# A three-stage layer on one core: outputs stored tile by tile, the split of the moved blocks one tile later, a fourth buffer for them

## The chip, the cores and the metric

The kernel runs on one core of one Trainium2 chip. The metric is device time in microseconds, the median of several runs. A profiled execution has a time of its own, and every duration below comes from that one execution.

The engines go by the names of the profile: PE multiplies matrices (PEld is its weight load), DVE, ACT and POOL work on tiles of 128 partitions, and SP issues the DMAs. An engine runs its instructions in program order and waits at one until the semaphores that it names are reached.

## What is computed

The input `x` is 8 sequences of 3072 tokens with 256 numbers each, 24576 tokens in all. Three stages follow each other:

```python
X = np.fft.rfft(x, axis=1)                  # stage 1: mix in the frequency domain, soft threshold
...                                         # Y = shrink(X @ (w_r + i w_i) + b), back by irfft
d = softmax over tokens of (x @ phi)        # stage 2: 32 slots, 8 experts
slot_out[e] = np.maximum(slot_input[e] @ w1[e], 0.0) @ w2[e]
x = c @ slot_out                            # c: softmax over the 32 slots, per token
h = x @ w_in                                # stage 3, per token: 256 -> 1024
sm = softmax(h)
solu = h * sm
ln = (solu - mean) / np.sqrt(var + 1e-06) * g_ln
out = ln @ w_out                            # 1024 -> 256
```

Everything is float32. The change lies in stage 3.

## The kernel before

Function `phase1` does stages 1 and 2 up to the slots, some 650 us of the span. Function `phase2` first makes the experts' outputs and multiplies them into `w_in`, so that one matrix `gst` leads from a token's 32 slot weights to its 1024 numbers `h`. Its main loop then goes over the tokens in 192 tiles of 128 tokens (`NI` = 192, four tiles to a group `j`, eight tiles to a new block `ct` of slot weights).

Nothing reorders the instructions: each engine gets them in the order in which the Python loop calls its helpers. Step `i` of the loop works on several tiles at once, and this is who does what to a tile `t`:

- `hmat` (PE, two matmuls): `h` of the tile, into the PSUM tile `hps` (three buffers).
- `rowmax` (DVE, L990), `expo` (ACT, L997), `umul` (DVE, L1005): row extremum, exponential, and `u = h * e`.
- `blocks` (L1016 to L1026): the product with `w_out` needs `u` transposed. DVE transposes the 32x32 blocks of `u` into `tb` (L1021, three buffers), and then four DMAs on SP's queue, 128 KB each, move blocks between partitions into `t2` (L1025, three buffers; the profile calls it `t`). This is done for tile `i+1` in step `i`.
- `uhi` (ACT takes six eighths, L1061; POOL the other two, L1062) makes the high part `uh` of the moved blocks, and `ulo` (POOL, two halves, L1071) the low part `ul = t2 - uh`. Both have four buffers. In step `i` they work on tile `i-1`.
- `vari` (ACT, L1081): sum of squares. `rstd` (POOL, four small instructions, L1106 to L1109): the inverse deviation, once for four tiles, in the last group once for each tile. It stands between the two halves of `ulo`.
- `prod` (PE): 16 matmuls with `uh`, then 8 with `ul`, into a PSUM tile that holds two tiles (two buffers). In step `i` it works on tile `i-3`.
- `outp` (ACT, L1123): scales the product of tile `i-6` into a quarter of `osb` (two buffers of four tiles). `store` (L1134) issues the 512 KB DMA of a whole group, with runs of 4 KB, two steps after the group's last `outp`. The last group goes out tile by tile from `outp` itself (L1126).
- `late_c`: in every eighth step four DMAs load the next `ct` (L855). `last_c`, between steps 20 and 33, splits the last sequence's slot weights once.

The last two tiles (`direct`) are transposed by PE and have no blocks moved.

On SP's queue the loop therefore has, per tile, four DMAs for `t2`; per four tiles one store; per eight tiles four loads of `ct`. SP issues them one after the other, and the four for tile `i+1` wait both for DVE's transposition and for the `t2` buffer, which `ulo` of an earlier tile gives free.

Of the kernel before, what the change touches and what calls it, by code (L numbers as in the profile page):

```python
# [8 lines left out]
F32 = mybir.dt.float32  # L9
# [26 lines left out]
def kernel(  # L36
# [32 lines left out]
    NI = T // 128  # L69
# [769 lines left out]
    def phase2(p2: ExitStack, pw: ExitStack):  # L839
# [87 lines left out]
        v = psl.rearrange("p d (o s) -> p d o s", o=1).to_broadcast([128, 2, 4, 32])  # L927
# [10 lines left out]
        for fh in range(2):  # L938
            o = gst.rearrange("p (b c j) -> p b c j", b=4, c=8)[:, :, 4 * fh:4 * fh + 4]
            v = pg[fh].rearrange("p (c j b) -> p b c j", c=4, b=4)  # L940
# [5 lines left out]
        def right(name, bufs, **k):  # L946
            return p2.enter_context(tc.tile_pool(name=name, bufs=bufs, side="right", **k))

        e_p = right("e_p", 2)
        u_p = right("u_p", 4)  # L950
# [20 lines left out]
        def hmat(i):  # L971
            if i >= NI:
                return
            j, k = divmod(i, 4)
            ps = ph_p.tile([128, DFF], F32, name="hps", tag="hps")
            for fh in range(2):
                mm(ps[:, 512 * fh:512 * fh + 512], ctt[j][:, 128 * k:128 * k + 128], (gstn if direct(i) else gst)[:, 512 * fh:512 * fh + 512])
            hps[i] = ps
# [7 lines left out]
        def rowmax(i):  # L986
            if i >= NI:
                return
            st, k = stats(i)
            DVE.tensor_reduce(out=st[:, 0, k:k + 1], in_=hps[i], op=ALU.min, axis=AX.X)  # L990

        def expo(i):
            if i >= NI:
                return
            st, k = stats(i)
            e = e_p.tile([128, DFF], F32, name="e", tag="e")
            ACT.activation(out=e, in_=hps[i], func=AF.Exp, bias=st[:, 0, k:k + 1], scale=-1.0, accum_out=st[:, 1, k:k + 1])  # L997
            et[i] = e

        def umul(i):  # L1000
            if i >= NI:
                return
            st, k = stats(i)
            u = u_p.tile([128, DFF], F32, name="u", tag="u")
            DVE.scalar_tensor_tensor(out=u, in0=hps.pop(i), scalar=1.0, in1=et.pop(i), op0=ALU.mult, op1=ALU.mult, accum_out=st[:, 2, k:k + 1])  # L1005
            ut[i] = u


        def direct(i):
            return i >= NI - 2  # L1010

        def gst_order():
            POOL.tensor_copy(out=gstn.rearrange("p (c j b) -> p b c j", c=8, b=4), in_=gst.rearrange("p (b c j) -> p b c j", b=4, c=8).bitcast(F32))
# [3 lines left out]
        def blocks(i):  # L1017
            if i >= NI or direct(i):
                return
            t = u_p.tile([128, DFF], F32, name="tb", tag="tb", bufs=3)  # L1020
            DVE.transpose(out=t, in_=ut[i])  # L1021
            t2 = u_p.tile([128, 4, 256], F32, name="t2", tag="t2", bufs=3)
            for a in range(4):
                z = slice(32 * a, 32 * a + 32)
                SP.dma_start(out=t2[:, a, :], in_=t[z].rearrange("i (b x) -> i b x", b=4))  # L1025
            t2t[i] = t2  # L1026

        def trans(i):
            if i >= NI or not direct(i):
                return  # L1030
            ps = ph_p.tile([128, 8, 128], F32, name="pu", tag="hps")
            for c in range(8):
                tp(ps[:, c, :], ut[i][:, 128 * c:128 * c + 128])
            ut[i, 0] = ps

        def parts(i):
            uh = u_p.tile([128, 8, 128], F32R, name="uh", tag="uh")
            ul = u_p.tile([128, 8, 128], F32R, name="ul", tag="ul")
            uht[i] = (uh, ul)
            return uh, ul  # L1040

        def direct_parts(i):
            if i >= NI or not direct(i):
                return
            uh, ul = parts(i)
            ps = ut.pop((i, 0))
            for n in range(2):
                z = slice(4 * n, 4 * n + 4)
                ACT.activation(out=uh[:, z, :], in_=ps[:, z, :], func=AF.Copy)
                DVE.tensor_tensor(out=ul[:, z, :], in0=ps[:, z, :], in1=uh[:, z, :].bitcast(F32), op=ALU.subtract)  # L1050
# [4 lines left out]
        def uhi(i):  # L1055
            if i < 0 or direct(i):
                return
            uh, ul = parts(i)
            v = t2t[i].rearrange("p a (c j) -> p c a j", c=8)
            w = uh.rearrange("p c (a j) -> p c a j", a=4)  # L1060
            ACT.activation(out=w[:, 0:HA], in_=v[:, 0:HA], func=AF.Copy)  # L1061
            POOL.tensor_copy(out=w[:, HA:8], in_=v[:, HA:8])  # L1062

        def ulo(i, n):
            if i < 0 or direct(i):
                return
            uh, ul = uht[i]
            z = slice(4 * n, 4 * n + 4)
            v = t2t[i].rearrange("p a (c j) -> p c a j", c=8)[:, z]
            w = uh[:, z, :].rearrange("p c (a j) -> p c a j", a=4)  # L1070
            POOL.tensor_tensor(out=ul[:, z, :].rearrange("p c (a j) -> p c a j", a=4), in0=v, in1=w.bitcast(F32), op=ALU.subtract)  # L1071
            if n:
                t2t.pop(i)


        def vari(i):
            if i >= NI:
                return
            st, k = stats(i)
            sq = e_p.tile([128, DFF], F32, name="sq", tag="sq", bufs=1)  # L1080
            ACT.activation(out=sq, in_=ut.pop(i), func=AF.Square, bias=st[:, 2, k:k + 1], scale=-float(DFF), accum_out=st[:, 3, k:k + 1])  # L1081
# [29 lines left out]
        o_todo = {}  # L1111

        def outp(i):
            if i < 0:
                return
            j, k = divmod(i, 4)
            b, r = divmod(j, 6)
            h, ah = divmod(r, 2)
            v = out.rearrange("(b h lm a) d -> b h lm a d", b=B, h=3, a=8)[b, h, :, 4 * ah:4 * ah + 4, :]
            if k == 0:  # L1120
                osb[0] = o_p.tile([128, 4, D], F32, name="osb", tag="osb")
            o = osb[0]
            ACT.activation(out=o[:, k], in_=pot.pop(i), func=AF.Copy, scale=stt[j][:, 4, k:k + 1])  # L1123
            if j == NG - 1:

                SP.dma_start(out=v[:, k, :], in_=o[:, k, :])  # L1126
            elif k == 3:
                o_todo[i + 2] = (v, o)


        def store(i):
            if i in o_todo:
                v, os2 = o_todo.pop(i)
                SP.dma_start(out=v, in_=os2)  # L1134
# [4 lines left out]
        def last_c(i):  # L1139
            d = [c_dram[B - 1, k].rearrange("h s x -> (h s) x") for k in range(2)]  # L1140
            if i == 20:
                cl[0] = o_p.tile([96, 1024], F32R, name="cl", tag="cl", bufs=1)
                cl[1] = o_p.tile([96, 1024], F32R, name="cl_h", tag="cl_h", bufs=1)
                SP.dma_start(out=cl[0].bitcast(F32), in_=d[0])
            elif i in (24, 26, 28, 30):
                z = slice(128 * (i - 24), 128 * (i - 24) + 256)
                POOL.tensor_copy(out=cl[1][:, z], in_=cl[0][:, z].bitcast(F32))
                POOL.tensor_tensor(out=cl[0][:, z], in0=cl[0][:, z].bitcast(F32), in1=cl[1][:, z].bitcast(F32), op=ALU.subtract)
            elif i == 33:
                SP.dma_start(out=d[0], in_=cl[1].bitcast(F32))  # L1150
                SP.dma_start(out=d[1], in_=cl[0].bitcast(F32))
# [3 lines left out]
        def late_c(i):  # L1155
            if i in c_todo:
                load_c(*c_todo.pop(i))
# [10 lines left out]
        expo(1)  # L1168
        umul(0)
        blocks(0)  # L1170
        for i in range(NI + 6):
            j, k = divmod(i, 4)
            hmat(i + 3)
            trans(i)
            rowmax(i + 2)
            umul(i + 1)
            blocks(i + 1)
            store(i - 6)
            late_c(i)
            last_c(i)  # L1180
            outp(i - 6)
            vari(i)
            expo(i + 2)
            direct_parts(i)
            if i <= NI:
                uhi(i - 1)
                ulo(i - 1, 0)
            rstd(i)
            if i <= NI:
                ulo(i - 1, 1)  # L1190
            if i == 40:
                gst_order()
            if k == 1:
                pieces(j + 2)
            prod(i - 3)
# [142 lines left out]
```

## Time and profile before

| | us |
|---|---|
| median of 3 runs | 1372.1 (1368.52 to 1372.83) |
| profiled execution, its own time | 1369.07 |
| its span, first to last instruction | 1367.2 |
| main loop: transposition of tile 1 to that of tile 189 | 679.4 (661.70 to 1341.11) |
| DVE busy from 900 to 1000 | 97.2 |

The span is 1.9 us shorter than the execution's time, and that time is 3.0 us under the median of the runs. The numbers of the page are one execution's; a share of busy time is an average, so the main loop is read by itself, from about 662 to 1341 us.

### The profile page before, as it was taken

The numbers are of one execution on the slowest core, as the hardware profiler recorded it, in microseconds if no ns is written. First come the engines' busy times: TensorE is split into PE (matmuls) and PEld (weight loads), VectorE is DVE, ScalarE is ACT, GpSimd is POOL, SyncE is SP. The second block draws the span as 40 slices with busy tenths as digits, with TensorE's granted clock in tenths as the row PEclk, the third lists the DMA queues.
The fourth block names the chain that finished last, engine by engine and source line by source line (L and its number), as shares of the span: only waits on it lengthen the run. The fifth ranks groups of instructions, "written<-read, shape, count | busy, mean of one in ns | idle before, by whom it ended". The sixth has DMA issues, their size and how long they took to land.

```text
span 1367.2 us, 30896 instructions
## 1 busy us (share of the span) xinstructions
PE 1267.8 (93%) x10784; PEld 1126.7 (82%) x10784; DVE 1204.8 (88%) x1691; ACT 1038.8 (76%) x2005; POOL 978.6 (72%) x1045
## 2 busy tenths in 40 slices
PE   6999999999999999878699989999999999999998
PEld 3888888888888788754588879889888898888998
DVE  7787989797888889765899999999999999999994
ACT  5567676666666665533799989999899899899996
POOL 5556575756565654321488999999989899899996
PEclk8999999999999999989899999999999999999999
DMA  8965463646455463169478787878878788887874
GB/s 264 301 202 168 128 201 102 201 116 191 134 161 153 143 178 136 62 208 305 101 179 217 188 215 196 206 194 214 200 195 202 195 200 214 199 207 193 201 192 129
DMA packets 190746, 252.70 MB, mean 185 GB/s; under 512 B 21504, under 2 KB 155392, under 8 KB 190592
## 3 DMA queue, kind: packets, MB, share of 16 engines
q1 hardware_dynamic: 190256, 249.57, 67.1%
q8 instruction: 85, 1.39, 0.4%
q10 hardware_dynamic: 336, 1.18, 0.3%
q14 instruction: 69, 0.57, 0.1%
HBM read 91.94 MB, written 59.11 MB: 110 GB/s over the span
## 4 chain that ended last, share of the span: by engine, by line
PE 33%; DVE 14%; POOL 13%; DMA 13%; issue 11%; SPq 10%; ACT 5%; POOLq 0%; ACTq 0%; DVEq 0%
DMA t<-tb 9%; POOL ul L1071 8%; PE pb L89 7%; SPq L1025 7%; PE po L89 5%; PE pm L89 5%; PE s L89 4%; PE xps L89 4%; PE pa L89 3%; SPq L855 2%; PE sps L92 2%; POOL uh L1062 2%; DVE u L1005 1%; DVE sl L313 1%; ACT uh L1061 1%
## 5 line engine op out<-in xcount | busy, mean ns | idle before, releaser
L1071 POOL TENSOR_TENSOR ul<-t,uh 128x512 fp32r<-128x512 f32 x380 | 487.3, 1301 | 31.1 <-ACT uh L1061 30.6
L89 PEld LDWEIGHTS po<-gw,uh 128*128 128x128 f32 x3072 | 385.9, 190 | 78.7 <-ACT osb L1123 69.6
L89 PE MATMUL po<-gw,uh 128*128 128x256 f32 x3072 | 405.0, 285 | 40.5 <-ACT osb L1123 40.0
L343 POOL TENSOR_TENSOR s<-yb,s 128x512 f32<-128x512 f32 x95 | 132.3, 1392 | 217.4 <-DVE s L342 190.2
L1021 DVE STREAM_TRANSPOSE tb<-u 128x1024 f32<-128x1024 f32 x190 | 236.7, 1246 | 7.0 <-DMA t<-tb 0.4
L1005 DVE SCALAR_TENSOR_TENSOR u<-hps,e 128x1024 f32<-128x1024 f32 x192 | 232.3, 1210 | 11.5 <-ACT e L997 11.3
L990 DVE TENSOR_REDUCE st<-hps 128x1 f32<-128x1024 f32 x192 | 227.7, 1186 | 2.1 <-PE hps L89 2.1
L1081 ACT ACTIVATE sq<-u,st 128x1024 f32<-128x1024 f32 x192 | 221.2, 1152 | 0.2 <-DVE u L1005 0.2
L997 ACT ACTIVATE e<-hps,st 128x1024 f32<-128x1024 f32 x192 | 214.2, 1116 | 7.6 <-DVE st L990 6.9
L89 PE MATMUL po<-gw,ul 128*128 128x256 f32 x1536 | 214.2, 282 | 1.0 <-POOL ul L1071 1.0
L89 PEld LDWEIGHTS po<-gw,ul 128*128 128x128 f32 x1536 | 196.5, 190 | 1.4 <-POOL ul L1071 1.4
L1061 ACT ACTIVATE uh<-t 128x768 fp32r<-128x768 f32 x190 | 160.5, 845 | 43.0 <-DMA t<-tb 40.6
L235 POOL TENSOR_TENSOR x<-xc,x 96x512 fp32r<-96x512 f32 x120 | 162.6, 1364 | 31.4 <-ACT x L234 31.3
L89 PE MATMUL hps<-gst,ct 128*128 128x512 f32 x380 | 119.7, 398 | 12.0 <-DVE u L1005 10.6
L261 ACT ACTIVATE asb<-s 96x512 f32<-96x512 f32 x112 | 66.7, 595 | 73.8 <-PE s L89 71.2
L89 PE MATMUL s<-x,df_h 96*96 96x512 f32 x240 | 104.6, 438 | 13.1 <-ACT x L234 4.6
L1062 POOL CAST uh<-t 128x256 fp32r<-128x256 f32 x190 | 76.9, 405 | 51.6 <-DMA t<-tb 48.3
L89 PEld LDWEIGHTS xps<-d_sb,apt 128*128 128x128 f32 x768 | 99.0, 193 | 13.6 <-issue 2.9
L89 PE MATMUL xps<-d_sb,apt 128*128 128x128 f32 x768 | 105.1, 280 | 1.8 <-DMA apt<-ad 1.5
L1123 ACT ACTIVATE osb<-po,st 128x256 f32<-128x256 f32 x192 | 89.6, 468 | 11.4 <-PE po L89 8.3
L297 DVE TENSOR_TENSOR xsum<-xps,xi 128x256 f32<-128x256 f32 x96 | 39.8, 414 | 52.4 <-ACT xh L296 46.3
L234 ACT ACTIVATE x<-xc 96x512 fp32r<-96x512 f32 x120 | 75.2, 626 | 12.5 <-DMA xc<-in_x_dram 12.3
(201 smaller groups left out, 2226.8 us busy)
## 6 DMA issues: line engine op xcount, KB each, us to landing
t<-tb SPq DMA_DIRECT2D x760, 128.0 KB, 2.8
apt<-ad SPq DMA_DIRECT2D x96, 256.0 KB, 4.2
out_dram<-osb SPq DMA_DIRECT2D x47, 512.0 KB, 3.7
xc<-in_x_dram SPq DMA_DIRECT2D x56, 384.0 KB, 4.0
ad<-asb SPq DMA_DIRECT2D x56, 384.0 KB, 3.5
ct<-c_dram SPq DMA_DIRECT2D x96, 128.0 KB, 3.8
wt<-in_moe_w_dram SPq DMA_DIRECT2D x21, 512.0 KB, 8.5
ws<-in_moe_w_dram SPq DMA_DIRECT2D x22, 256.0 KB, 6.3
```

The costliest lines, as they stand in the source:

```text
L89: PE.matmul(out=out, lhsT=lhsT, rhs=rhs, start=start, stop=stop)
L235: POOL.tensor_tensor(out=lo, in0=t, in1=hi.bitcast(F32), op=ALU.subtract)
L343: (DVE if (b, t) == (B - 1, NT - 1) else POOL).tensor_tensor(out=s, in0=yb, in1=s, op=ALU.subtract)
L990: DVE.tensor_reduce(out=st[:, 0, k:k + 1], in_=hps[i], op=ALU.min, axis=AX.X)
L997: ACT.activation(out=e, in_=hps[i], func=AF.Exp, bias=st[:, 0, k:k + 1], scale=-1.0, accum_out=st[:, 1, k:k + 1])
L1005: DVE.scalar_tensor_tensor(out=u, in0=hps.pop(i), scalar=1.0, in1=et.pop(i), op0=ALU.mult, op1=ALU.mult, accum_out=st[:, 2, k:k + 1])
L1021: DVE.transpose(out=t, in_=ut[i])
L1025: SP.dma_start(out=t2[:, a, :], in_=t[z].rearrange("i (b x) -> i b x", b=4))
L1061: ACT.activation(out=w[:, 0:HA], in_=v[:, 0:HA], func=AF.Copy)
L1062: POOL.tensor_copy(out=w[:, HA:8], in_=v[:, HA:8])
L1071: POOL.tensor_tensor(out=ul[:, z, :].rearrange("p c (a j) -> p c a j", a=4), in0=v, in1=w.bitcast(F32), op=ALU.subtract)
L1081: ACT.activation(out=sq, in_=ut.pop(i), func=AF.Square, bias=st[:, 2, k:k + 1], scale=-float(DFF), accum_out=st[:, 3, k:k + 1])
```

## The change

Three things change, all in the main loop of `phase2`. The `t2` blocks get four buffers. A finished tile is stored by itself, one step after its `outp`, with a 128 KB DMA of 1 KB runs. And `uhi` and `ulo` work on tile `i-2` in step `i`; `prod` stays at tile `i-3`.

```diff
-            t2 = u_p.tile([128, 4, 256], F32, name="t2", tag="t2", bufs=3)
+            t2 = u_p.tile([128, 4, 256], F32, name="t2", tag="t2", bufs=4)
...
                 SP.dma_start(out=v[:, k, :], in_=o[:, k, :])
-            elif k == 3:
-                o_todo[i + 2] = (v, o)
+            else:
+                o_todo[i + 1] = (v[:, k, :], o[:, k])
...
             direct_parts(i)
-            if i <= NI:
-                uhi(i - 1)
-                ulo(i - 1, 0)
+            if i <= NI + 1:
+                uhi(i - 2)
+                ulo(i - 2, 0)
             rstd(i)
-            if i <= NI:
-                ulo(i - 1, 1)
+            if i <= NI + 1:
+                ulo(i - 2, 1)
```

SP's queue in the middle of the loop, before (the rows `t<-tb` are the four DMAs of one tile, `out_dram<-osb` a store, `ct<-c_dram` the load of slot weights):

```order
L1025 DMA t_11632<-tb 128x1x256 x4
L1025 DMA t_11680<-tb 128x1x256 x4
L1025 DMA t_11730<-tb 128x1x256 x4
L1025 DMA t_11779<-tb 128x1x256 x4
L1134 DMA out_dram<-osb 128x1024
L855 DMA ct<-c_dram 32x1024 x4
L1025 DMA t_11838<-tb 128x1x256 x4
L1025 DMA t_11886<-tb 128x1x256 x4
```

And in the changed kernel, again around a load of `ct`:

```order
L1025 DMA t_13412<-tb 128x1x256 x4
L1134 DMA out_dram<-osb 128x256
L1025 DMA t_13462<-tb 128x1x256 x4
L1134 DMA out_dram<-osb 128x256
L855 DMA ct<-c_dram 32x1024 x4
L1025 DMA t_13521<-tb 128x1x256 x4
L1134 DMA out_dram<-osb 128x256
L1025 DMA t_13570<-tb 128x1x256 x4
L1134 DMA out_dram<-osb 128x256
```

Every tile's four DMAs are now followed by a store: 188 stores of 128 KB (four more of the last group stay as they were) in place of 47 of 512 KB, 141 more instructions on SP.

ACT's queue over two steps, before (`sq` squares tile `i`, whose transposed blocks have a number four above that of its `u`; `uh` splits the tile before it, so that `sq` of `u_9677` stands with `uh` from `t2_9631`):

```order
L1081 ACTIVATE sq_9742,st_9474<-u_9677,st_9474 128x1024
L997 ACTIVATE e_9744,st_9675<-hps_9672,st_9675 128x1024
L1061 ACTIVATE uh_9746<-t2_9631 128x768
L1123 ACTIVATE osb_9686<-po2_9647,st_9269 128x256
L1081 ACTIVATE sq_9795,st_9675<-u_9726,st_9675 128x1024
```

And in the changed kernel:

```order
L1081 ACTIVATE sq_9743,st_9471<-u_9677,st_9471 128x1024
L997 ACTIVATE e_9745,st_9675<-hps_9672,st_9675 128x1024
L1061 ACTIVATE uh_9747<-t2_9581 128x768
L1123 ACTIVATE osb_9687<-po2_9647,st_9263 128x256
L1081 ACTIVATE sq_9797,st_9675<-u_9727,st_9675 128x1024
```

The order of kinds is the same; the split beside the same `sq` takes blocks that are one tile older. POOL's `uh` and `ul` move with it, past one `rstd`, while PE's and DVE's queues keep their order.

## Rows read from the trace of the kernel before

**Rows 1.** The page: busy us (share of the span) xinstructions; chain that ended last.
```profile
PE 1267.8 (93%) x10784; PEld 1126.7 (82%) x10784; DVE 1204.8 (88%) x1691; ACT 1038.8 (76%) x2005; POOL 978.6 (72%) x1045
DMA t<-tb 9%; POOL ul L1071 8%; PE pb L89 7%; SPq L1025 7%; PE po L89 5%; PE pm L89 5%; PE s L89 4%; PE xps L89 4%; PE pa L89 3%; SPq L855 2%; PE sps L92 2%; POOL uh L1062 2%; DVE u L1005 1%; DVE sl L313 1%; ACT uh L1061 1%
```

**Rows 2.** Busy us by stretch, 900 to 1000: engines, PEclk, DMA share, GB/s.
```profile
900.00:1000.00 100.00, 92.54 (x716) 86.72 (x715) 97.22 (x112) 92.08 (x167) 90.27 (x111) 1.00 0.81 201
```

**Rows 3.** Timeline of DVE, 655 to 700: start us, us, engine, line, operation.
```profile
661.70 1.25 DVE L1021 STREAM_TRANSPOSE tb<-u 128x1024 f32<-128x1024 f32 x1
...
697.06 1.25 DVE L1021 STREAM_TRANSPOSE tb<-u 128x1024 f32<-128x1024 f32 x1
```

**Rows 4.** Timeline of all engines, end of the loop, 1338 to 1368.
```profile
1341.11 1.25 DVE L1021 STREAM_TRANSPOSE tb<-u 128x1024 f32<-128x1024 f32 x1
...
1354.18 0.19 POOL L1106 TENSOR_SCALAR st<-st 128x1 f32<-128x1 f32 x1
...
1355.50 1.27 POOL L1071 TENSOR_TENSOR ul<-t,uh 128x512 fp32r<-128x512 f32 x1
...
1356.83 0.74 PE L89 MATMUL po<-gw,ul 128*128 128x256 f32 x4 [0.71 <-POOL ul L1071]
```

**Rows 5.** Waits in the loop, 662 to 1341: us in total, times, longest us.
```profile
ACT uh L1061 <- DMA t<-tb: 40.6, 37, 2.4
PE po L89 <- ACT osb L1123: 39.7, 36, 2.3
...
DVE u L1005 <- ACT e L997: 10.5, 19, 1.1
```

**Rows 6.** Waits of SP's own queue, 662 to 1341.
```profile
SPq L1025 <- POOL uh L1062: 93.5, 105, 2.4
```

**Rows 7.** Issues by line, L1025 (with its landing), L1134, L1126: duration ns min/median/max.
```profile
L1025 SPq DMA_DIRECT2D t<-tb x753: 542/602/1865, 661.5 to 1340.8; - x189
...
DMA to landing us min/median/max: 2.5/2.8/4.9
...
L1134 SPq DMA_DIRECT2D out_dram<-osb x44: 589/592/607, 704.5 to 1327.4; - x44
...
L1126 SPq DMA_DIRECT2D out_dram<-osb x4: 333/360/404, 1358.1 to 1364.3; - x4
```

**Rows 8.** Timeline of SP's queue, 777 to 807.
```profile
776.48 3.40 SPq L1025 DMA_DIRECT2D t<-tb  x5
779.92 0.59 SPq L1134 DMA_DIRECT2D out_dram<-osb  x1
780.61 2.43 SPq L855 DMA_DIRECT2D ct<-c_dram  x4
783.20 5.16 SPq L1025 DMA_DIRECT2D t<-tb  x8
788.41 0.60 SPq L1150 DMA_DIRECT2D c_dram<-cl_h  x1
789.05 0.43 SPq L1151 DMA_DIRECT2D c_dram<-cl  x1
789.64 7.12 SPq L1025 DMA_DIRECT2D t<-tb  x8
796.80 0.59 SPq L1134 DMA_DIRECT2D out_dram<-osb  x1
```

**Rows 9.** Timeline of SP's queue, 686 to 705: a load with no store ahead.
```profile
690.43 1.94 SPq L855 DMA_DIRECT2D ct<-c_dram  x4
```

**Rows 10.** Timeline of POOL, 1038 to 1048: one tile with `rstd`, then plain ones.
```profile
1037.93 1.30 POOL L1071 TENSOR_TENSOR ul<-t,uh 128x512 fp32r<-128x512 f32 x1
...
1041.13 1.30 POOL L1071 TENSOR_TENSOR ul<-t,uh 128x512 fp32r<-128x512 f32 x1
1042.37 0.40 POOL L1062 CAST uh<-t 128x256 fp32r<-128x256 f32 x1
...
1045.22 0.41 POOL L1062 CAST uh<-t 128x256 fp32r<-128x256 f32 x1
```

## The prediction

> **What bounds the kernel now.** I read the page first, to see which engines are busy at all: PE and DVE lead, and the chain that ended last passes through the moves of blocks, POOL's low parts and SP's queue [rows 1]. All parts of the change lie in the main loop, so the loop is read alone. There DVE is busy 97.22 us of 100, PE 92.54, ACT 92.08, POOL 90.27 [rows 2]: four engines nearly full, and DVE the fullest.
>
> DVE's own pace comes from its timeline near the start of the loop, where nothing stops it: ten tiles between the transpositions at 661.70 and 697.06, 3.536 us each [rows 3]. The last transposition begins at 1341.11 [rows 4], so 188 tiles took 679.41 us, where 188 x 3.536 = 664.8 would do. The loop loses 14.6 us over DVE's floor, and that is all a change of waits can win here.
>
> Who takes these 14.6 us? The waits show ACT held 37 times, 40.6 us in all, at the high part, for blocks that have not landed; DVE then waits for ACT's exponential, 10.5 us; PE waits for ACT's output copy [rows 5]. SP, which issues the moves, waits itself in turn 93.5 us at the first move of a tile, put down to POOL [rows 6]: with three buffers for the blocks, tile i+1 can't be moved before the low part of tile i-2 is done. So there is a ring of three tiles: POOL frees a buffer, SP issues four moves, they land, ACT and POOL split them. A load or a store on SP's queue makes it longer than three steps, and all engines slip.
>
> **What the change does to this ring.** The fourth buffer and the later split go together: the blocks get one step (3.536 us) more to land, and the ring has four steps. Its length now: four issues up to the start of the last, 3 x 0.65 = 1.9, landing 2.8 [rows 7], POOL's part of the split 1045.22 - 1042.37 = 2.85, and in every fourth tile `rstd` between the halves, 1041.13 - 1037.93 - 1.30 = 1.90 more [rows 10]. That is 7.6 to 9.5 us, to which a store and a load of `ct` on SP, from 779.92 to 783.20, add 3.3 [rows 8]: up to 12.8 against 10.6 in three steps (so it stalls), and against 14.1 in four (so it doesn't). The longest single waits, 2.4 for ACT and 1.1 for DVE [rows 5], are smaller than the step that is won. These stalls go, and I cost the ring at nothing from here on.
>
> **What is late next: SP itself.** Count what SP must issue per tile, back to back, each duration being that of the issue on SP and not of the transfer.
> - Four moves. The median issue is 602 ns, the longest 1865 [rows 7]. Where SP runs without a pause, eight take from 783.20 to 788.41, 2.61 per tile; but over the three runs of moves from 776.48 to 796.80, which hold the long issues too, 21 take 3.44 + 5.21 + 7.16 = 15.81, 3.01 per tile [rows 8]. I take 2.76, nearer to the clean end, since few issues are long (the median is the clean one).
> - One store. After a move it takes 592 ns, 44 times with hardly any spread; with the gap to the next issue 0.64. Runs of 1 KB right after a move are not in the trace; the four stores of 1 KB runs take 333 to 404 ns, but behind idle time or other stores [rows 7]. So 0.38 to 0.64 per tile. I take 0.64, because what stands ahead of an issue seems to set its price: of two like transfers in a row the one behind moves took 0.60 and the one behind it 0.43 [rows 8], and the new stores all stand right behind moves.
> - A load of `ct` per eight tiles: 2.59 from its start to the next move behind a 512 KB store [rows 8], 1.94 without a store ahead [rows 9]; per tile 0.24 to 0.32, taken 0.28.
>
> The sum is 2.76 + 0.64 + 0.28 = 3.68 us per tile; before it is 2.76 + 0.16 + 0.32 = 3.24, which DVE's 3.536 covers. So the queue that had 0.3 us to spare per tile has 0.14 us too little. The bounds: 2.61 + 0.38 + 0.24 = 3.23, well under the floor, and 3.01 + 0.64 + 0.32 = 3.97.
>
> **The sum.** Stores begin at step 7, so some 182 tiles run at SP's pace: 182 x (3.68 - 3.536) = 26.2 us over the floor. Not all of it shows, for SP may first fall behind: `tb` has three buffers, so a move must have landed when DVE transposes the third tile after it, 3 x 3.536 - 1.25 = 9.36 us after the transposition ended; issue and landing need 2.6 + 2.8 = 5.4, which leaves 3.9 us. ACT, which needs the blocks in that same step, gives no more. So 22.3 us over the floor, where before it was 14.6: +7.7.
>
> The end of the kernel loses a little. In the last group `rstd` runs for each tile, and it now stands one tile later beside the split: the second half of the last tile's low part has one `rstd` more ahead of it, which took from 1354.18 to 1355.50, 1.3 us, and PE waited for that half already [rows 4]. +1.3.
>
> The product stands where it was, and its operands come one step later. PE is busy 3.3 us per tile (92.54 of 100 at 3.6 [rows 2]) and wants the second half of `ul` for the last 4 of 24 matmuls, so by estimate 2.5 us after the product's start; POOL ends that half 2.6 us after ACT's split, so about then, and 1.9 later in a tile with `rstd` [rows 10]. `h` of a tile is wanted only at DVE's next step but one, by estimate 3 us after PE is done with the product before it, so a wait of 1 to 2 us moves PE but not DVE: nothing, while that cover holds. If ACT is late on top, it costs what the third rival says. The 141 stores more carry the same bytes, in runs of 1 KB; the DMA share of 0.81 [rows 2] leaves room.
>
> Together 1369.07 + 7.7 + 1.3 = 1378.1 for the profiled execution. That one stands 3.0 under the median of the runs (1372.1), so I predict 1381.
>
> **The rivals.**
> - *SP keeps up: faster.* If a store of 128 KB costs SP its 0.38 and not 0.64, the demand is 2.76 + 0.38 + 0.24 = 3.38, under 3.536, and DVE's floor is reached but for a few waits: -14.6 + 3 + 1.3 = -10.3, that is 1362. For it: the four cheap stores [rows 7]. Against it: 44 of 44 stores behind a move took 592. The Trainium skill has a rule by which it comes out so: "DMA: Bandwidth & Descriptors", section "Anatomy of one DMA — SWDGE (gpsimd) path", puts the sequencer's dispatch of a DMA at about 50 ns and the making of descriptors at little more, though for DMAs that POOL issues; by that an extra store costs SP next to nothing, and this rival's 1362 follows. The rows here, 592 ns on SP, don't agree with it.
> - *The two waits are equal: no change.* If the demand is 3.60 to 3.65 (fewer long issues than in the stretch that I read), 182 x (0.064 to 0.114) - 3.9 = 7.7 to 16.8 over the floor stand for the 14.6 of now: with the end -5.6 to +3.5, about 1372.
> - *PE behind the split: slower still.* If ACT's copies come late in the tiles with `rstd`, PE's cover of 3 us is used up and the next `h` is late for DVE: 47 such tiles by 0.3 to 0.5 us, 14 to 24 us on top of what SP costs, some 1397. It decides once PE's waits for `ul` are longer than 3 us; before they total 0.2 us in the loop, and PE's waits are for ACT's copies [rows 5]. Little speaks for it.
>
> The Trainium skill, "DMA: Bandwidth & Descriptors", section "Rules for kernel authors", advises to issue a DMA early and wait for it late, so that its fixed cost is covered. ACT's 40.6 us [rows 5] agree that this cover was short; by that rule alone the sum would be the first rival's 1362, and it says nothing of a queue that issues without a pause.
>
> **How the numbers follow.** SP as the bound 0.5 (1376 to 1392, with the demand at 3.66 to 3.74), SP keeps up 0.26 (1357 to 1367), equal 0.18, PE behind the split 0.06. The range of 1360 to 1393 leaves out the last rival and the lower part of the first, and some of the forecast's upper end (3.97 is the row with cl's stores in it, which come once). Faster or slower counts from 0.3%, 4 us, about what a measurement of this kernel can tell from no change: faster 0.27, same 0.2, slower 0.53. The sides forecast and not forecast both hold much, so: the likeliest case alone is 1376 to 1392.
>
> **What would show it.** Right: SP's queue without a pause in the loop, nearly no waits of SP for POOL; a store row of about 592 ns; DVE waiting for `tb`'s moves or ACT for landed blocks, at a steady 3.6 to 3.7 us per tile, beginning some 30 tiles into the loop; the waits of ACT gone before that. Wrong: stores of 350 to 400 ns and SP waiting for DVE's transposition (the first rival), or PE waiting at `ul` for POOL (the third). Should SP's long issues be caused by the 512 KB stores, they go with them, and the demand falls by up to 0.15 towards the second rival.

## The result, and the profile after

The changed kernel takes 1385.7 us (median of 4 runs, 1384.86 to 1386.7) beside 1370.3 (4 runs) for the kernel before: a ratio of 1.011, interval 1.0088 to 1.0133. It is 15.4 us, 1.1%, slower. The forecast was 1381, 8.9 us over the median of 1372.1 that it started from; with a fourth run that median is 1370.3. The profiled execution took 1384.86 us with a span of 1383.1, against 1369.07 and 1367.2 before.

The page of the changed kernel (busy us, share of the span, instructions; then the chain that ended last) answers to [rows 1]:

```profile
PE 1268.7 (92%) x10784; PEld 1138.5 (82%) x10784; DVE 1201.7 (87%) x1691; ACT 1054.6 (76%) x2005; POOL 976.1 (71%) x1045
SPq L1025 9%; POOL ul L1071 9%; DMA t<-tb 8%; PE pb L89 6%; PE pm L89 5%; PE po L89 5%; PE s L89 5%; PE xps L89 3%; PE pa L89 3%; DVE st L990 2%; ACT uh L1061 2%; PE sps L92 2%; DMA xc<-in_x_dram 1%; SPq L1134 1%; DVE sl L313 1%
```

The engines do the same work in nearly the same busy time (PEld's and ACT's grew by 1 to 1.5%), and the span is longer. SP's issue of the moves has become the first entry of the chain. The page alone doesn't say why: SP's queue isn't counted as an engine, and the share of every engine on the first line is the same as before or a point lower.

The stretch 900 to 1000 (PE, PEld, DVE, ACT, POOL, then granted clock, DMA share, GB/s), which answers to [rows 2]:

```profile
900.00:1000.00 100.00, 92.61 (x712) 88.79 (x710) 93.30 (x108) 91.95 (x161) 87.09 (x108) 0.98 0.79 196
```

DVE does 108 instructions where it did 112, busy 93.30 us and not 97.22. The transfers move less per second than before (196 GB/s, 201 before) and the DMA engines' share fell from 0.81 to 0.79, so they aren't what got full.

The waits in the main loop, 662 to 1355 (us in total, times, longest us), for [rows 5]:

```profile
PE po L89 <- POOL ul L1071: 51.4, 44, 1.9
POOL ul L1071 <- ACT uh L1061: 32.4, 51, 4.5
DVE tb L1021 <- DMA t<-tb: 26.8, 23, 2.9
ACT uh L1061 <- DMA t<-tb: 23.5, 21, 2.8
```

DVE, the engine that sets the floor, now waits for the moves out of `tb`: 26.8 us, nearly its whole loss of 27.5 (table below). And the waits of SP's own queue in that stretch, for [rows 6]:

```profile
SPq L1025 <- POOL ul L1071: 19.1, 43, 1.0
SPq L1025 <- POOL uh L1062: 8.1, 17, 1.3
```

The 93.5 us for POOL's `uh` are down to 8.1. What is left comes in pieces of some 0.45 us (19.1 / 43, 8.1 / 17), and these aren't pauses: in this view a semaphore's update that falls inside the row of an issue counts as the end of a wait. The gaps between SP's issues on its timeline are the better measure. From tile 8 to tile 189 the longest in the changed kernel is 0.49 us, and only 12 of 988 are over 0.25; the kernel before has 46 of more than half a us there, 60.6 us in all. What SP does instead, on its timeline from 1100 to 1140 (start us, us, line, transfer), for [rows 8]:

```profile
1101.05 2.49 SPq L1025 DMA_DIRECT2D t<-tb  x4
1103.58 0.61 SPq L1134 DMA_DIRECT2D out_dram<-osb  x1
1104.35 2.50 SPq L1025 DMA_DIRECT2D t<-tb  x4
1106.89 0.60 SPq L1134 DMA_DIRECT2D out_dram<-osb  x1
1107.60 1.78 SPq L855 DMA_DIRECT2D ct<-c_dram  x4
1109.54 2.75 SPq L1025 DMA_DIRECT2D t<-tb  x4
1112.34 0.60 SPq L1134 DMA_DIRECT2D out_dram<-osb  x1
1113.10 3.34 SPq L1025 DMA_DIRECT2D t<-tb  x4
1116.48 0.60 SPq L1134 DMA_DIRECT2D out_dram<-osb  x1
```

Each row starts within 0.2 us of the end of the one before: SP issues without a pause. Four clean moves take 2.49 and the store 0.60, so a clean tile takes 3.3 us; a long issue among the four adds 0.8 (the row at 1113.10), a load of `ct` 1.9. The issues by line over the loop (duration ns min/median/max), for [rows 7]:

```profile
L1025 SPq DMA_DIRECT2D t<-tb x752: 542/603/1851, 662.7 to 1354.9; - x188
L1134 SPq DMA_DIRECT2D out_dram<-osb x180: 340/596/1498, 690.5 to 1352.3; - x180
```

From the loop's rows the demand per tile is 2.79 for the moves with the short wait instructions ahead of them, 0.66 for the store with its gap, 0.24 for `ct` (1.94 per eight tiles), 3.69 us in all. Where the time went, from the transpositions at 661.39 and 1353.67 (timeline of DVE) and [rows 3, 4]:

| | before | after | forecast |
|---|---|---|---|
| loop, tile 1 to 189 | 679.4 | 692.3 (+12.9) | +7.7 |
| of it over DVE's floor of 664.8 | 14.6 | 27.5 | 22.3 |
| last transposition to the end of the span | 26.1 | 29.4 (+3.3) | +1.3 |

The span grew by 15.9: 12.9 and 3.3, less 0.3 at the start. The last column is the forecast, the first two come from one execution each.

How far the transposition of a tile has slipped behind DVE's floor (its start, less that of tile 1, less 3.536 us per tile, on DVE's timeline), for the two kernels and three of the experiments below:

| tile | before | after | e1 | e3 | e9 |
|---|---|---|---|---|---|
| 24 | 0.0 | 0.0 | 0.0 | 0.0 | 0.0 |
| 48 | 6.1 | 5.9 | 5.9 | 2.1 | 3.7 |
| 96 | 8.8 | 13.2 | 5.9 | 2.1 | 5.4 |
| 144 | 12.6 | 22.2 | 5.9 | 2.1 | 5.9 |
| 189 | 14.6 | 27.5 | 5.9 | 2.1 | 7.0 |

Up to tile 48, in the stretch in which `last_c` works, before and after lose about the same, though not by the same wait (see the part on why the prediction was right). Then the changed kernel slips on, 21.6 us in 141 tiles or 0.153 per tile on average (0.12 to 0.19 between the rows of the table), where the demand of 3.69 exceeds 3.536 by 0.154. On a queue without pauses these two must agree: that accounts for the time, and what tests the cause are the experiments in which the number of stores changes (e1, e3, e4).

### The profile page after: what moved, and what is told of

Its sections match the earlier page's. It is cut to its first block, busy times and chain, and to the rows that moved or that the text cites. A ratio compares the mean times of both kernels' runs of the same rounds, so it can differ in the third digit from the quotient of the medians.

```text
span 1383.1 us, 31087 instructions
## 1 busy us (share of the span) xinstructions
PE 1268.7 (92%) x10784; PEld 1138.5 (82%) x10784; DVE 1201.7 (87%) x1691; ACT 1054.6 (76%) x2005; POOL 976.1 (71%) x1045
## 4 chain that ended last, share of the span: by engine, by line
PE 32%; DVE 15%; POOL 13%; issue 12%; SPq 11%; DMA 10%; ACT 6%; POOLq 0%; ACTq 0%; DVEq 0%
SPq L1025 9%; POOL ul L1071 9%; DMA t<-tb 8%; PE pb L89 6%; PE pm L89 5%; PE po L89 5%; PE s L89 5%; PE xps L89 3%; PE pa L89 3%; DVE st L990 2%; ACT uh L1061 2%; PE sps L92 2%; DMA xc<-in_x_dram 1%; SPq L1134 1%; DVE sl L313 1%
## 5 line engine op out<-in xcount | busy, mean ns | idle before, releaser
L89 PEld LDWEIGHTS po<-gw,uh 128*128 128x128 f32 x3072 | 393.2, 191 | 21.3 <-ACT uh L1061 6.3
L89 PE MATMUL po<-gw,uh 128*128 128x256 f32 x3072 | 398.9, 283 | 3.0 <-ACT uh L1061 2.8
L89 PE MATMUL po<-gw,ul 128*128 128x256 f32 x1536 | 226.3, 284 | 55.2 <-POOL ul L1071 55.1
L1021 DVE STREAM_TRANSPOSE tb<-u 128x1024 f32<-128x1024 f32 x190 | 236.6, 1245 | 33.9 <-DMA t<-tb 26.8
L234 ACT ACTIVATE x<-xc 96x512 fp32r<-96x512 f32 x120 | 75.1, 626 | 12.7 <-DMA xc<-in_x_dram 12.4
```

The source lines that it names most:

```text
L89: PE.matmul(out=out, lhsT=lhsT, rhs=rhs, start=start, stop=stop)
```

## The experiments

By content, the theories are these. **Q**: SP's issue queue is the bound; what counts is how many DMAs SP issues per tile, against DVE's floor. **R**: it is the stores' runs of 1 KB, or their traffic, and not their number. **P**: PE stands too close behind the later split, and its 51 us of waits for `ul` are the loss. **L**: of the two parts that were meant to give time, the later split is what takes the stalls away, and the fourth buffer alone gains little. **B**, against it: the ring of three buffers makes the stalls, and the buffer takes most of them away. "Loop" below is us per tile from tile 1 to 189, "end" the time from the last transposition to the end of the span; both come from the profiled execution.

| kernel | median us (range, runs) | ratio to before, interval | loop | end |
|---|---|---|---|---|
| after | 1385.7 (1384.9 to 1386.7, 4) | 1.011, 1.0088 to 1.0133 | 3.682 | 29.4 |
| e1: after, stores as before | 1363.8 (1361.0 to 1365.6, 6) | 0.9947, 0.9932 to 0.9961 | 3.567 | 29.5 |
| e2: e1 with runs of 1 KB | 1361.9 (1359.9 to 1362.9, 4) | 0.9932, 0.9915 to 0.9949 | 3.568 | 29.5 |
| e3: after, a store per two tiles | 1358.5 (1357.3 to 1360.0, 4) | 0.9906, 0.9888 to 0.9925 | 3.547 | 29.4 |
| e4: after, two stores per tile | 1510.2 (1508.7 to 1511.6, 2) | 1.1016, 1.0989 to 1.1042 | 4.356 | 29.0 |
| e5: after, product one tile later | 1385.0 (1383.0 to 1388.8, 4) | 1.0117, 1.0095 to 1.0139 | 3.705 | 29.3 |
| e6: before, a store per tile | 1391.0 (1387.7 to 1392.7, 4) | 1.0155, 1.0135 to 1.0175 | 3.731 | 27.2 |
| e7: e3, last split taken forward | 1357.7 (1356.6 to 1361.1, 6) | 0.9917, 0.9900 to 0.9935 | 3.544 | 27.9 |
| e8: after, stores issued by ACT | 1399.6 (1396.2 to 1403.1, 2) | 1.0221, 1.0189 to 1.0253 | 3.767 | 31.4 |
| e9: before, fourth buffer alone | 1358.6 (1357.3 to 1361.4, 4) | 0.9909, 0.9875 to 0.9944 | 3.573 | 25.6 |
| e10: before, later split alone | 1531.7 (1528.5 to 1535.6, 4) | 1.1177, 1.1139 to 1.1214 | 4.438 | 32.9 |
| e11: before, buffer and a store per two tiles | 1353.6 (1351.8 to 1355.5, 4) | 0.9887, 0.9854 to 0.9919 | 3.544 | 25.2 |
| e12: before, buffer and a store per tile | 1385.7 (1383.4 to 1389.5, 4) | 1.0119, 1.0088 to 1.0151 | 3.710 | 26.4 |

### e1 and e2: the stores undone, and the stores undone but for their runs

```diff
-            else:
-                o_todo[i + 1] = (v[:, k, :], o[:, k])
+            elif k == 3:
+                o_todo[i + 2] = (v, o)
```

and e2 besides, so that a store of four tiles has runs of 1 KB:

```diff
-                osb[0] = o_p.tile([128, 4, D], F32, name="osb", tag="osb")
+                osb[0] = o_p.tile([128, 4, D + 8], F32, name="osb", tag="osb")[:, :, 0:D]
```

> Four buffers and the later split of the changed kernel, but the stores of the kernel before: 512 KB per four tiles, two steps after the group. Theory Q (SP's issue queue is the bound, through the 141 stores more): SP's demand falls back to about 3.2 us per tile, the loop runs at DVE's floor of 3.54 to 3.56 us per tile, SP waits again for DVE's transposition, and the time is 1355 to 1364 us, faster than both kernels. Theory P (the product stands too close behind the split, PE waits for POOL's low part): nothing of that is undone, so the time stays at 1380 to 1388. Theory R (stores in runs of 1 KB load the DMA engines, moves land later): the runs are 4 KB again, 1355 to 1364 as well.

> As the run with four buffers, later split and group stores, but a row of the output buffer is padded by 8 numbers, so that the same 512 KB store is made of runs of 1 KB: as few issues as before the change, as short runs as after it. Theory Q: within 3 us of that run, 1355 to 1367, the store's issue at 0.59 to 0.65 us. Theory R: the short runs cost what they cost in the changed kernel, 1378 to 1388. Theory P: 1380 to 1388.

Without the 141 extra stores the kernel is faster than before, 1363.8 us; its loop loses nothing after tile 48. SP has pauses again (59 gaps of more than half a us from tile 8 on, 53.1 us in all), which end with DVE's transposition or when POOL frees a buffer. Waits of SP's queue in e1, 662 to 1340:

```profile
SPq L1025 <- DVE tb L1021: 38.2, 57, 1.0
SPq L1025 <- POOL uh L1062: 30.9, 50, 1.8
```

With runs of 1 KB the time is 1361.9, not above that of e1: R falls as far as the runs go. The bytes are the same in all three kernels, so the slowdown hangs on the tile-by-tile stores; that it is their number, e3 and e4 show.

### e3 and e4: half as many stores, and twice as many

e3 stores two tiles with 256 KB, e4 cuts the store of a tile into two halves of the partitions:

```diff
-            else:
-                o_todo[i + 1] = (v[:, k, :], o[:, k])
+            elif k % 2:
+                o_todo[i + 1] = (v[:, k - 1:k + 1, :], o[:, k - 1:k + 1])
```

```diff
-                SP.dma_start(out=v, in_=os2)
+                for z in (slice(0, 64), slice(64, 128)):
+                    SP.dma_start(out=v[z], in_=os2[z])
```

> The changed kernel with a store for two tiles (256 KB, runs of 2 KB) in place of one for each: half of the stores, one step after the pair. Theory Q: SP's demand is 2.78 + 0.32 + 0.24 = 3.34 us per tile, under DVE's floor of 3.536, so all of the loss goes and not half of it: 1356 to 1367. Theory R: half of the loss goes, about 1370 to 1378. Theory P: 1380 to 1388.

> The changed kernel with each tile's store cut into two of 64 partitions: the same bytes and the same runs of 1 KB, 188 issues more on SP. Theory Q: SP's demand rises from 3.69 by 0.45 to 0.64 us per tile, 184 tiles, so the time is 1468 to 1505 us. Theories P and R: bytes, runs and the place of the product are the same, 1380 to 1392.

P and R miss both results. Q has e3 right and e4 5 us above its range. The dose fits a threshold. With the terms read from the changed kernel (2.79 + 0.24 + 0.66 per store) SP's demand is 3.36 us per tile in e3, 3.69 in the changed kernel and 4.35 in e4; the loops take 3.547, 3.682 and 4.356. Under DVE's 3.536 SP's issues cost nothing, above it each store costs its whole 0.66: e4's second store adds 4.356 - 3.682 = 0.674, the same bytes in the same loop. SP's gaps say the same: e3 has 26 of more than half a us from tile 8 on, e4 one, of 0.50. Halving the stores takes away not half of the loss but all of what came after tile 48. In e4 the waits of 662 to 1340 are those of the changed kernel, more than four times as large:

```profile
DVE tb L1021 <- DMA t<-tb: 123.3, 116, 3.8
ACT uh L1061 <- DMA t<-tb: 101.2, 106, 3.7
```

And e3 in the stretch 900 to 1000, where DVE is at its floor (third pair of numbers):

```profile
900.00:1000.00 100.00, 94.72 (x739) 91.00 (x738) 98.99 (x115) 97.10 (x171) 92.79 (x114) 1.00 0.81 205
```

With twice as many stores as e1, e3 is 5.3 us faster. That isn't SP's issue queue, which has room in both. The difference arises between tiles 24 and 48 (5.9 and 2.1 us lost in the table of slips). What e1 has and e3 has not is a wait of ACT for a store that should free `osb` (662 to 1340; two of these waits, 4.1 us, lie between tiles 24 and 48):

```profile
ACT osb L1123 <- DMA out_dram<-osb: 9.3, 11, 2.9
```

So smaller stores give the output buffer back sooner. Whether that is the reason stays open: e2 has 18.3 us of the same wait and is no slower than e1.

### e5: the product one tile later

```diff
-            prod(i - 3)
+            prod(i - 4)
```

> The changed kernel with the product one tile later too (tile i-4 in step i), so that it stands as far behind the split as before the change. Theory Q: PE's waits for POOL's low part, 51 us in the changed kernel, go, and the time doesn't follow, since SP issues no faster: 1383 to 1389, SP still without a pause. Theory P: the distance is what was lost, so a good part of the 15 us comes back: 1368 to 1378.

PE's wait for `ul`, 51.4 us in the changed kernel, is no longer among the waits of 662 to 1340, yet the time is the same, 1385.0. DVE's wait for the moves has stayed:

```profile
DVE tb L1021 <- DMA t<-tb: 32.0, 38, 2.4
ACT uh L1061 <- DMA t<-tb: 26.6, 31, 2.3
```

P falls: PE's wait is a symptom off the path.

### e6: the stores alone

```diff
-            elif k == 3:
-                o_todo[i + 2] = (v, o)
+            else:
+                o_todo[i + 1] = (v[:, k, :], o[:, k])
```

> The kernel before with the stores tile by tile alone: three buffers, split and product where they were. Theory Q: SP's demand is that of the changed kernel, 3.65 to 3.70 us per tile, and without the later split there is no step of reserve to be late in, so it is as slow or slower: 1383 to 1402. Theory P: split and product are as far apart as before, so the time stays within 5 us of the kernel before.

The stores alone cost 1.6%, more than the three parts together. With three buffers the blocks come late for ACT as well, 58.3 us in 662 to 1340, before [rows 5] 40.6:

```profile
ACT uh L1061 <- DMA t<-tb: 58.3, 53, 3.2
PE po L89 <- ACT osb L1123: 53.3, 50, 3.1
DVE u L1005 <- ACT e L997: 24.0, 32, 1.1
```

### e8: the stores issued by ACT

```diff
-                SP.dma_start(out=v, in_=os2)
+                ACT.dma_start(out=v, in_=os2)
```

> The changed kernel with each tile's store issued by ACT in place of SP. Theory Q: SP's demand falls by 0.64 to 3.05 us per tile and SP waits again for DVE and POOL; ACT, 3.31 us busy per tile, takes on the issue: at 0.35 to 0.65 us it needs 3.66 to 3.96 per tile and becomes the bound, so 1385 to 1440. Theories P and R: 1380 to 1392, as the changed kernel, with SP's row count alone different.

SP is relieved: in 662 to 1340 it waits 115.5 us at the first move of a tile.

```profile
SPq L1025 <- POOL uh L1062: 115.5, 117, 3.0
SPq L1025 <- DVE tb L1021: 39.6, 64, 1.9
```

But the time is 1399.6, the loop 3.767. The issues of line L1134, by count and duration:

```profile
L1134 ACTq DMA_DIRECT2D out_dram<-osb x188: 338/339/411, 682.1 to 1388.2; - x188
```

An issue takes 0.34 us here, and by estimate it takes it from ACT, which was busy 92 of 100 us [rows 2]: 92% of 3.6 us and 0.34 more are 3.65 us per tile before any wait. DVE waits for ACT's exponential, 25.0 us in 662 to 1340 where [rows 5] have 10.5. An issue queue with room is no help on an engine without room.

### e9 and e10: the buffer alone, the later split alone

e9 is the kernel before with one line changed, e10 is e1 with three buffers:

```diff
-            t2 = u_p.tile([128, 4, 256], F32, name="t2", tag="t2", bufs=3)
+            t2 = u_p.tile([128, 4, 256], F32, name="t2", tag="t2", bufs=4)
```

```diff
-            t2 = u_p.tile([128, 4, 256], F32, name="t2", tag="t2", bufs=4)
+            t2 = u_p.tile([128, 4, 256], F32, name="t2", tag="t2", bufs=3)
```

> The kernel before with four buffers for the moved blocks alone (split a step earlier than in the changed kernel, group stores). Theory B (the ring of three buffers made the waits of before): most of the gain of the run with later split, four buffers and group stores is there, 1358 to 1364, and SP's waits for POOL are gone. Theory L (the time to land made them: a load or a store ahead on SP makes the blocks come after ACT wants them): ACT's waits for landed blocks stay near 40 us and the time at 1365 to 1373.

> The later split and group stores with three buffers. Theory B: the ring of three is as short as before, so the time stays at 1366 to 1376. Theory L: the step that is won for landing takes ACT's waits away, and with the end 3 us longer the time is 1359 to 1365; SP then waits for POOL at nearly every tile, which costs nothing.

The buffer alone gives 1358.6 us, 5 better than buffer and later split together (e1). Waits of SP's queue in e9, 662 to 1340:

```profile
SPq L1025 <- DVE tb L1021: 52.7, 76, 1.4
SPq L1025 <- POOL ul L1071: 13.4, 33, 0.8
SPq L1025 <- POOL uh L1062: 12.4, 32, 0.7
```

B has its time and L does not. SP hardly waits for POOL to free a buffer any more (93.5 us for `uh` in [rows 6], 12.4 here) but for DVE's transposition, so it issues a tile as soon as there is one. ACT's waits for landed blocks have hardly shrunk, and yet DVE's loss behind tile 48 is 3.3 us instead of 8.5 (the table of slips). Of the engines' waits of e9 in that stretch:

```profile
ACT uh L1061 <- DMA t<-tb: 36.9, 26, 2.8
PE po L89 <- ACT osb L1123: 30.2, 27, 2.7
...
DVE u L1005 <- ACT e L997: 3.0, 7, 1.1
```

L falls by the time, though not by the waits: ACT's 36.9 us hardly matter any more, since ACT mostly catches up before DVE needs it (3.0 us instead of 10.5).

The later split with three buffers is the worst of all, 4.438 us per tile, and both expectations (1359 to 1376) missed it by more than 150 us: a buffer is now given free one step later. Waits of SP's queue, then of the engines, in 662 to 1340 of e10:

```profile
SPq L1025 <- POOL uh L1062: 185.6, 84, 3.0
```

```profile
ACT osb L1123 <- DMA out_dram<-osb: 148.2, 32, 5.9
PE po L89 <- ACT osb L1123: 91.1, 35, 4.1
DVE u L1005 <- ACT e L997: 65.2, 35, 3.4
```

The first wait is the ring of three tiles. The others show how it spreads: the store stands on SP's queue behind moves that wait, ACT waits for the `osb` that the store should free, and PE and DVE wait for ACT.

### e7, e11, e12: what a better version keeps

e7 is e3 with the split of tile 189 done in step 190, together with that of tile 188:

```diff
-            if i <= NI + 1:
+            if i < NI - 1:
...
+            if i == NI - 2:
+                uhi(NI - 3)
+                ulo(NI - 3, 0)
+                ulo(NI - 3, 1)
```

> The run with a store for two tiles, with one thing more: the split of the last moved tile (189) is done in step 190 together with tile 188, and not a step later. All theories: the loop stays at 3.55 us per tile. If the 3.3 us that the end of the changed kernel has grown (26.1 to 29.4 us behind the last transposition) come from the split's place behind the last direct tile on ACT, they go: 1354 to 1357 us, the end 26 to 27. If they come from POOL's inverse deviations, the end stays at 28.5 to 29.5 and the time at 1357 to 1360.

The end shrinks by 1.5 us (29.4 to 27.9), half of what the later split had added, which is between the two expectations; the median of 1357.7 can't be told from e3's 1358.5.

e11 has e9's buffer and e3's stores, e12 has e9's buffer and the changed kernel's stores, both with the split where it was before.

> The kernel before with the fourth buffer for the moved blocks and one 256 KB store per two tiles; the split stays one step behind the moves. If only the count of issues on SP against DVE's floor matters (2.79 for the moves, 0.33 for half a store, 0.24 for the load of ct: 3.36 against 3.536 us per tile), the loop is 2 to 7 us over the floor, as with either edit's best, and the end is that of the kernel with the buffer alone, 25.6 us behind the last transposition and not 29.4: 1354 to 1358. If stores that come more often need the later split, because the blocks are wanted one step earlier, ACT's waits grow and the loop is over 10 us above the floor: 1362 or more.

> The kernel before with the fourth buffer and a store per tile; the split stays one step behind the moves. So it is the changed kernel without the later split. If SP's issue queue sets the pace, the loop is that of the changed kernel, 27 us over the floor (3.68 us per tile), and only the end is shorter, by 2 to 4 us: 1382 to 1384. If the later split is worth something while SP is the bound, the loop is that of the kernel before with the stores alone, 33 to 37 us over the floor: 1389 to 1391.

e11 is the fastest kernel of the study: 1353.6 us, 1.1% faster than before. In 900 to 1000 DVE is at its floor; from 662 to 1340 it waits 1.4 us for ACT's exponential; and the end is 25.2 us long.

```profile
900.00:1000.00 100.00, 96.70 (x745) 91.86 (x744) 99.00 (x115) 95.75 (x173) 92.91 (x117) 0.98 0.81 206
```

e12 is as slow as the changed kernel, 1385.7 us beside 1385.7: once SP is the bound, the later split is worth nothing, within some 3 us. Its loop of 3.710 lies between the two expectations, but its profiled execution was the slowest of its four (1389.5), so the difference to 3.682 stays open.

## Why the prediction was right

**The bound: right.** The forecast named SP's issue queue, with 3.68 us per tile; the rows show 3.69, the loop behind tile 48 takes 3.689, and e1, e3 and e4 move the loop as the count of issues says. The time came out 4.7 us over the forecast, though the change was off by 6.5 (+15.4, not +8.9): the kernel before has a median of 1370.3 and not of 1372.1, and that 1.8 is luck. Of the terms, the moves came to 2.79 (2.76 said), the store to 0.66 (0.64), `ct` to 0.24 (0.28). The store's price was the choice that decided the sign: 0.64 by the 44 stores behind moves, not 0.38 by the four cheap ones [rows 7]. The median of the new stores, 596 ns, confirms it. The reason that I gave, that what stands ahead sets the price, is too simple: in e4 the second store of a tile, right behind the first, isn't cheap. The row holds both (start us, us):

```profile
1105.67 1.26 SPq L1135 DMA_DIRECT2D out_dram<-osb  x2
```

By that reason it should have been about 0.6 and 0.4. As for `ct`, it got cheaper because its second issue no longer stands behind a 512 KB store (the last part has the numbers).

**The signs that were named: all there.** SP without a pause, stores of about 592 ns, DVE waiting for `tb`'s moves and ACT for landed blocks, a steady 3.6 to 3.7 us per tile from about tile 30 on, with no slip at all up to tile 24.

**The loss in the loop: +12.9, not +7.7.** The mechanism held, and two terms of its sum were off in size. SP makes no pause from tile 8 on, so the whole loss is SP's. The first store, right behind the moves of tile 8, starts at 690.53 (690.5 in the row of L1134 above). The stores right behind the moves of tiles 27 and 188, on SP's timeline:

```profile
762.39 0.60 SPq L1134 DMA_DIRECT2D out_dram<-osb  x1
1355.58 0.61 SPq L1134 DMA_DIRECT2D out_dram<-osb  x1
```

The first term is the demand: from tile 8 to tile 188, 180 tiles took 1355.58 - 690.53 = 665.05 us, 3.695 each, which is 28.6 over DVE's floor, where I had 26.2. The second is the reserve, by which SP may fall behind before DVE feels it. The transpositions of the three tiles start at 686.14, 753.32 and 1350.14 (timeline of DVE). So SP had fallen 4.7 us further behind by tile 27 (9.07 less 4.39 from transposition to store), before DVE's first slip at tile 28, and I had taken off 3.9. But the reserve wasn't kept to the end: the last load of `ct` is issued at 1287, the demand without it is 3.45, under DVE's floor, and SP catches up. At tile 188 it is only 1.0 us further behind than at tile 8, so 28.6 - 1.0 = 27.5 show, not 26.2 - 3.9 = 22.3. The reserve had an error of its own, too: landing counts from the start of an issue, as the ring's sum has it (1.9 + 2.8), so 2.6 + 2.8 counts the last issue twice. Put right, it is 4.6, close to the 4.7 measured.

"These stalls go, and I cost the ring at nothing" holds for the changed kernel only because SP covers what is left of them. In the stretch of tiles 24 to 48 DVE now waits for SP's moves (730 to 840):

```profile
DVE tb L1021 <- DMA t<-tb: 5.3, 4, 2.9
```

The kernel before loses about as much there, but waits 4.3 us for ACT's exponential. In e1, where SP has room, 5.9 us are lost there as well, in waits for PE's `h` (2.4) and ACT's exponential (1.7) above all. So four buffers and the later split don't take away all stalls; what causes these was not taken apart.

**The end: +3.3, not +1.3.** I counted one `rstd` more on POOL, but a whole split more stands there. POOL's rows at the end of the changed kernel, with PE's last product (timeline, 1362 to 1374):

```profile
1364.35 1.29 POOL L1071 TENSOR_TENSOR ul<-t,uh 128x512 fp32r<-128x512 f32 x1
1365.73 0.19 POOL L1106 TENSOR_SCALAR st<-st 128x1 f32<-128x1 f32 x1
...
1367.05 1.28 POOL L1071 TENSOR_TENSOR ul<-t,uh 128x512 fp32r<-128x512 f32 x1
1368.27 0.40 POOL L1062 CAST uh<-t 128x256 fp32r<-128x256 f32 x1
1368.63 1.29 POOL L1071 TENSOR_TENSOR ul<-t,uh 128x512 fp32r<-128x512 f32 x1
1370.01 0.19 POOL L1106 TENSOR_SCALAR st<-st 128x1 f32<-128x1 f32 x1
...
1371.34 1.26 POOL L1071 TENSOR_TENSOR ul<-t,uh 128x512 fp32r<-128x512 f32 x1
1372.65 0.75 PE L89 MATMUL po<-gw,ul 128*128 128x256 f32 x4 [1.19 <-POOL ul L1071]
```

Where `rstd` runs for each tile, POOL works without a pause, and a tile takes it 1368.63 - 1364.35 = 4.28 us. Behind the last transposition it now does nine halves of low parts, before seven: one tile more. The last half ends 1371.34 + 1.26 - 1353.67 = 18.9 us behind that transposition, before 1355.50 + 1.27 - 1341.11 = 15.7 [rows 4], so 3.2 of the 3.3 us are here; most of the rest of the 4.28 is that POOL began its first half behind the transposition 0.9 us sooner. The kernels that keep the split where it was end 25.2 to 27.2 us behind the last transposition (e6, e9, e11, e12), those that move it 29.0 to 29.5 but for e7 and the slower e8 and e10.

**"The fourth buffer and the later split go together": wrong.** The ring needs the buffer: with it alone (e9) the loop loses 7.0 us instead of 14.6. A later split doesn't shorten the ring; it holds each buffer for one step more, and without the buffer that is ruinous (e10). I had added its step to the time that the blocks have to land, which is true, and not to the time that the buffer is held. With the buffer there and room on SP, the later split costs 5 us (e1 beside e9, e3 beside e11), mostly at the end. That this didn't hurt the forecast is luck: SP covered it all.

**PE's wait: right.** 51 us of it, longest 1.9, under the cover of 3 us that I gave it; e5 takes it away and nothing changes.

**The rivals.** That SP keeps up fell with the 596 ns. The Trainium skill ("DMA: Bandwidth & Descriptors", section "Anatomy of one DMA — SWDGE (gpsimd) path") puts a dispatch at about 50 ns, for DMAs that POOL issues. For SP that isn't borne out: a move or store mostly takes 0.54 to 0.60 us, and e4 pays 0.674 for one more per tile. That the two waits are equal fell too: it wanted a demand of 3.60 to 3.65. PE behind the split didn't happen.

The later split itself loses 5 us with four buffers and room on SP, and 162 without the fourth buffer (e10, beside 1369.5 for the kernel before). The rule of the Trainium skill to issue a DMA early and wait for it late ("DMA: Bandwidth & Descriptors", section "Rules for kernel authors"), read alone, would have made it a gain.

**The long issues.** I had left open whether the 512 KB stores cause them, in which case they would go. They didn't: 40 of the 752 moves still take more than 0.66 us and add 0.13 per tile; before it was 39 of 753.

## What to carry to other kernels

Count what each queue issues per period of the loop, at the duration of an issue behind its usual neighbour, and set the sum against the busiest engine: below it an extra DMA was free here, above it each cost its full price, for half a tile (e4) as for a whole one. Where a wait is a ring of buffers, a buffer opens it; moving the consumer later gives time to the transfer but holds the buffer longer. And work that is moved one step later adds up to a whole step of its engine to the tail, where nothing hides it.

## What the runs showed of the hardware

The price of an issue depends on what stands ahead of it, though by no simple rule. The second load of `ct` took about 1.05 us where a 512 KB store stands ahead of the loads (the kernel before, e1, e2) and 0.42 behind one of 128 KB. The one store of `cl_h` took 0.60 behind moves in the kernel before and 0.43 behind a store in the changed one; but in e4 a half store behind a half store took 0.60. A 128 KB store took 0.60 on SP right behind moves and 0.34 on ACT's queue, which issues no moves and belongs to another engine.

"Perfetto Trace Analysis" of the Trainium skill, section "What "DMA-bound" means", names the state seen here, an issuing engine whose track is solid with DMA windows, and says that large descriptors are what matters then. The first agrees with SP's timeline after. The second no run here tests in that state: e2, whose SP has room, shows only that the issue of a 512 KB store takes 0.60 us with runs of 1 KB as with runs of 4 KB (e1), while one issue more or less per tile changes the time.

The long issues on SP fall together with 16 KB packets on another DMA queue, which the profile calls instruction. In the changed kernel's loop 36 issues take 0.9 to 1.9 us, some 18 us apart, and 33 of them lie within 2 us of one of that queue's 39 packets. In the kernel before there are packets at 987.0, 1003.7 and 1023.4 us and long issues at 986.8, 1003.9 and 1023.7. On the page of the changed kernel that queue is (packets, MB, share):

```profile
q8 instruction: 85, 1.39, 0.4%
```

That is a coincidence in time; its cause was not tried.
